# Attention in a fused layer kernel: how far its VectorE work is written ahead of TensorE, when its output is loaded, and k ahead of q

## The chip, the cores and the metric

The kernel runs on one core of a Trainium2 chip. A core has TensorE (PE, matrix products into the PSUM banks), VectorE (DVE), ScalarE (ACT), GpSimd (POOL), a sync engine (SP) whose queue starts most transfers, and 16 DMA engines. Each engine works through its own queue in order; they meet at semaphores. The metric is the device time of one execution in microseconds, the median of several runs.

## The reference

With x of 2048 x 512 (one batch), D = 512, 32 heads of 16, F = 1792, all in float32:

```python
xn = layernorm(x)
q, k, v = split(xn @ wqkv)
idx = pos[:, None] - 2 * arange(8)[None, :]
logits = einsum("hsd,hswd->hsw", q, k[idx]) * 0.25
logits = where(idx >= 0, logits, -1e9)
o = einsum("hsw,hswd->hsd", softmax(logits), v[idx])
s = o @ wo
h = relu(xn @ w1 + b1) ** 2
out = x + s * silu(h @ w2 + b2)
```

So each position looks at eight keys only: its own and every second one before it, back to 14. That part is done on VectorE; the four matrix products are done on TensorE.

## The kernel before

**Precision.** A matrix product takes three passes: operands are split into a high part (a rounded copy, ScalarE, `high`) and a low part (a subtraction on VectorE or GpSimd, `low`), and high x high, high x low and low x high are added in PSUM (`PASSES`, L34). A product of 128 x 512 by 512 x 512 is 12 matmuls.

**First phase (L522-642).** Sixteen tiles of 128 rows are normalised (`mean`, `spread`, `norm`), transposed (`trans`), split (`lowx`) and multiplied by q, k and v weights (`qkv(t, s)`; s = 0, 1, 2 for q, k, v). `evacuate` (L472) copies a product to an SBUF tile; after every second tile the pair is written to DRAM (`sq`, `sk`, `sv`) and `done_tiles` notes how many tiles there are, with q and k under one name. The FFN weights are loaded (`load_w`, L364) and split (`split_w`, L373, low part on GpSimd) as the phase goes on.

**Second phase (L645-806).** Four chunks c of 512 rows; in each, 14 steps f over F: `up(c, f)` (12 matmuls to a bank `ph`, of which `psH` has two), relu and two squares on ScalarE, `lowh(f)` (the subtraction `h<-ph,h` on VectorE, which frees the bank), and two steps later `down(pb, f, j)` for the chunk's four row tiles (12 matmuls). `gate` adds b2 and takes silu, `out_product` multiplies the attention's output by wo, `finish` multiplies and adds x and stores.

**Attention (L221-343).** A generator, `stream`, in 8 units u of 256 rows. For a unit: four times `qk` (multiply, reduce), `soft_a`, the exponential on ScalarE, `soft_b`, four times `av` (multiply, reduce into the v tile), `store` to DRAM (`so`). In its order qk of unit u stands before av of unit u - 1. There is one buffer each for q, k and v, loaded from DRAM on ScalarE's queue (`load_u`, L199); v of the last unit uses k's buffer.

**Order.** The program is one list per engine, laid out when it is built. Two planned clocks, `clock["PE"]` and `clock["V"]`, grow by prices (L43, L55-64). `pump(margin)` (L348) writes attention instructions into VectorE's list as long as their price fits under `clock["PE"] + margin`; `not_before` moves VectorE's clock to a time that it has to wait for. `defer` and `flush` (L213-219) put the load of a unit into ScalarE's list when TensorE's clock passes a time: `BEHIND` = 5000 ns after VectorE's clock for q, k, v and for the exponential, and at least `LAND` after the tiles were done; `LOAD` is how long the plan takes a load to need (`there`, L241). In the second phase the margin is `ROOM` = 1000 for chunks 1 to 3 and -500 for chunk 0 (L770), and -500 wherever `pump()` stands alone.

**The attention's output.** `load_o(u)` (L660) starts four transfers of unit u's output into the one buffer `oq`, on SP. If the unit isn't written yet, its loop (L661-663) pumps with a margin large enough to write it all, there and then. It stands at f == 7 for unit 2c and at f == 12 for unit 2c + 1 (L755, L765). `trans_o` (VectorE transpose, ScalarE copy) follows for the chunk's first two tiles at f == 10, for the other two at f == 3 of the next chunk; `lowo` one step later, `out_product` at the chunk's end (L772) and at f == 5 and 6. In the last chunk all is done at its end (L787-806).

At a chunk's end (L772-786): two output products, the last two `down` groups, `up(c+1, 0)`, `up(c+1, 1)`, then on VectorE the four gates, `lowh(0)`, `lowh(1)`, and only then `pump()`.

Of the kernel before, what the change touches and what calls it, by code (L numbers as in the profile page):

```python
# [14 lines left out]
P = 128  # L15
# [26 lines left out]

MATMUL, TRANSPOSE, DVE_FIXED, SLACK, LATE, ROOM = 227, 150, 170, 500, 3000, 1000  # L43

BEHIND, LAND, LOAD = 5000, 6000, 9500


@with_exitstack
def body(ctx: ExitStack, tc: tile.TileContext, x, wqkv, wo, w1, b1, w2, b2, out):
# [59 lines left out]
    def high(hi, lo, src):  # L109
        A.activation(hi, src, AF.Copy)  # L110
# [43 lines left out]
    def wq_parts(s, kt):  # L154
        return wq[s][:, 0, kt], wq[s][:, 1, kt], raws[s, kt]

    load_x(0)
    load_wq(0, 0)
    load_x(1)
    for kt in range(1, KT):  # L160
        load_wq(0, kt)
    for kt in (0, 2):
        load_wq(1, kt, "pr")
    load_x(2)
# [30 lines left out]

    done_tiles = dict(qk=[0, {}], v=[0, {}])
    done_units = [0]
# [23 lines left out]
    def attention():  # L221
# [5 lines left out]
        def qk(u, s):  # L227
            i0 = 2 * s
            yield from there("k", u)
            q, k, L = tiles["q", u], tiles["k", u], Ls[u]  # L230
            yield 2350
# [240 lines left out]
    def evacuate(t, s, ps):  # L472
# [4 lines left out]
        if t % 2:  # L477
            r0 = (t - 1) * P + (0 if s == 0 else HALO)
            dst = (sq, sk, sv)[s][:, r0:r0 + UP, :].rearrange("g (p e) c -> p g (e c)", e=2)
            dma(dst, stgs[s].rearrange("p g e c -> p g (e c)"))  # L480
            done = done_tiles["qk" if s < 2 else "v"]
            done[0] = t + (s > 0)
            done[1][t // 2] = clock["PE"]
# [40 lines left out]
    moments(0, sts[0])  # L524
    high(*wq_parts(0, 0))
    norm(0)
# [6 lines left out]
    moments(1, sts[1])  # L533
    low(*wq_parts(0, 0), V)

# [5 lines left out]
    for kt in range(1, KT):  # L541
        split(*wq_parts(0, kt), V)
    high(xt[0][:, 0], None, x0.rearrange("p (k n) -> p k n", k=KT))
    ps = psA("pq0_0")
    for kt in range(KT):
        if kt == KT - 1:
            trans(1)
        PE.matmul(ps, x0[:, kt * P:(kt + 1) * P], raws[0, kt], start=kt == 0, stop=kt == KT - 1)
# [12 lines left out]
    spread(3)  # L561
    qkv(0, 1, lambda: highs(2, 0))
    trans(2)
# [3 lines left out]
    mean(4)  # L567
    qkv(1, 1, lambda: highs(2, 2))
    lows(2, 2)
    spread(4)  # L570
    constants()
    trans(3)
# [86 lines left out]

    def load_o(u):  # L660
        while done_units[0] <= u:  # L661
# [52 lines left out]
    for c in range(NCH):  # L714
        last = c == NCH - 1
        pb = [psA(f"pb{c}_{j}") for j in range(TPC)]
        t0 = c * TPC
        for f in range(2, NF):
            if c == 0:
# [54 lines left out]
        pump()  # L774
        if not last:
            for i in range(2):
                for j in range(TPC):
                    down(pb, NF - 2 + i, j)
                pump()
            for i in range(2):  # L780
                up(c + 1, i)
            for j in range(TPC):
                gate(c, j, pb)
            lowh(0)
            lowh(1)
            pump()
        else:  # L787
# [40 lines left out]
```

## Time and profile before

| | us |
|---|---|
| median of 3 runs | 519.23 |
| lowest, highest | 518.88, 520.03 |
| profiled execution | 518.02 |
| its span (first to last instruction) | 516.2 |

The profile is of one execution. Its page gives busy shares by engine; the timeline lists instructions with start, duration, count and, in brackets, the idle time before them with what ended it; the windows give busy time, the granted TensorE clock and the DMA share for stretches of the span. Tile names follow the program: `ph` and `h` of the FFN, `pb` its second product, `pw` the output product, `pr`, `L`, `pv` of the attention, `oq`, `pT`, `oT` of its output. All instructions carry line 78, that of the helper that records them.

### The profile page before, as it was taken

Reading aid. Unit: us, or ns where it says so; the run is one execution under the profiler, and the core shown is the slowest. Engines: PE = TensorE matmul, PEld = TensorE weight load, DVE = VectorE, ACT = ScalarE, POOL = GpSimd, SP = SyncE. Lnnn points to the kernel's source line nnn. Section 1 sums busy time; section 2 is a strip of 40 time slices with the busy share of each in tenths; the row PEclk is TensorE's granted clock in tenths of the full one; section 3 lists DMA queues with packets and bytes.
Section 4 is the critical chain, followed back from the end, with each engine's and each line's share of the span. In section 5 each row is a group of like instructions: output and inputs, shape, how many; then the busy total and the mean of one; then the engine's idle time right before and its main releaser. Section 6 shows DMA issues by size and latency. Waiting matters only on the chain.

```text
span 516.2 us, 5907 instructions
## 1 busy us (share of the span) xinstructions
PE 493.7 (96%) x2174; PEld 403.8 (78%) x2174; DVE 425.1 (82%) x350; ACT 218.8 (42%) x397; POOL 91.9 (18%) x121
## 2 busy tenths in 40 slices
PE   8999999999999999999999999999999999949965
PEld 5788888878887888888888888888888888738854
DVE  6419992999999999976999994899998399956956
ACT  5974573852343565217242413722431642403212
POOL 1321153531002697001030000102000101100000
PEclk9999999999999999999999999999999999979998
DMA  8989869869997936443061440708046320320222
GB/s 290 278 271 362 250 184 332 245 235 326 327 290 199 290 116 224 149 171 115 9 215 60 152 163 1 234 16 255 5 153 253 104 81 22 132 81 2 81 81 83
DMA packets 48088, 88.27 MB, mean 171 GB/s; under 512 B 5324, under 2 KB 31932, under 8 KB 45244
## 3 DMA queue, kind: packets, MB, share of 16 engines
q1 hardware_dynamic: 43740, 54.34, 34.0%
q10 hardware_dynamic: 4320, 33.56, 18.4%
q8 instruction: 17, 0.28, 0.2%
q14 instruction: 11, 0.09, 0.1%
HBM read 57.94 MB, written 27.32 MB: 165 GB/s over the span
## 4 chain that ended last, share of the span: by engine, by line
PE 62%; DVE 19%; DMA 6%; issue 5%; ACT 5%; POOL 1%; SPq 0%; ACTq 0%; DVEq 0%; POOLq 0%
PE pb L78 24%; PE ph L78 23%; PE pq L78 10%; PE pw L78 5%; DVE pv L78 4%; DVE pr L78 3%; DVE L L78 3%; DVE v L78 3%; DMA xb<-xn 2%; DMA sx<-xt 2%; DVE z L78 1%; DVE h L78 1%; DMA w1r<-in_B_w 1%; ACT scratch L78 1%; DVE oT L78 1%
## 5 line engine op out<-in xcount | busy, mean ns | idle before, releaser
L78 PE MATMUL pb<-w,h 128*128 128x512 f32 x672 | 160.9, 389 | 2.5 <-DVE h L78 2.5
L78 PEld LDWEIGHTS pb<-w,h 128*128 128x128 f32 x672 | 126.0, 188 | 29.1 <-DVE h L78 2.9
L78 PE MATMUL ph<-xU,w 128*128 128x512 f32 x504 | 122.3, 394 | 8.4 <-DVE h L78 8.4
L78 ACT ACTIVATE ph<-ph,b1t 128x512 f32<-128x512 f32 x56 | 37.0, 660 | 204.1 <-PE ph L78 193.2
L78 PEld LDWEIGHTS ph<-xU,w 128*128 128x128 f32 x504 | 95.5, 190 | 29.5 <-DVE h L78 9.7
L78 PE MATMUL pq<-wq,xt 128*128 128x512 f32 x432 | 99.0, 390 | 0.8 <-DVE xt L78 0.8
L78 PEld LDWEIGHTS pq<-wq,xt 128*128 128x128 f32 x432 | 80.9, 188 | 18.5 <-DVE xt L78 1.3
L78 DVE TENSOR_TENSOR pr<-k,q 128x2048 f32<-128x2048 f32 x32 | 75.7, 2366 | 13.5 <-DMA k<-sk 13.2
L78 DVE TENSOR_TENSOR pv<-v,L 128x2048 f32<-128x2048 f32 x32 | 74.3, 2322 | 0.6
L78 DVE TENSOR_REDUCE L<-pr 128x128 f32<-128x2048 f32 x32 | 72.9, 2279 | 0.7
L78 DVE TENSOR_REDUCE v<-pv 128x256 f32<-128x2048 f32 x32 | 72.9, 2280 | 0.6
L78 DVE TENSOR_TENSOR h<-ph,h 128x512 fp32r<-128x512 f32 x56 | 38.1, 684 | 34.7 <-ACT ph L78 34.7
L78 POOL TENSOR_TENSOR z<-z,xr 128x512 f32<-128x512 f32 x12 | 19.3, 1618 | 221.1 <-DVE z L78 163.3
L78 PE MATMUL pw<-wot,oT 128*128 128x512 f32 (+2 forms) x216 | 46.8, 371 | 1.4 <-DVE oT L78 1.4
L78 PEld LDWEIGHTS pw<-wot,oT 128*128 128x128 f32 x216 | 38.0, 188 | 8.9 <-DVE oT L78 1.8
L78 PE MATMUL ph<-xT,w 128*128 128x512 f32 x168 | 40.6, 391 | 0.5 <-DVE h L78 0.5
L78 ACT ACTIVATE stg<-pq 128x512 f32<-128x512 f32 x48 | 28.1, 594 | 28.5 <-PE pq L78 25.8
L78 PEld LDWEIGHTS ph<-xT,w 128*128 128x128 f32 x168 | 31.5, 188 | 7.5 <-DVE h L78 0.9
L78 POOL TENSOR_TENSOR w<-w1r,w 128x512 fp32r<-128x512 f32 x14 | 25.2, 1798 | 63.0 <-DMA rwo<-in_A_wo 46.6
L78 ACT ACTIVATE h<-ph 128x512 fp32r<-128x512 f32 x56 | 33.6, 601 | 1.8
L78 ACT ACTIVATE ph<-ph 128x512 f32<-128x512 f32 x56 | 33.3, 595 | 0.0
L78 PE MATMUL pq<-wq,xT 128*128 128x512 f32 x132 | 32.4, 400 | 0.0
(64 smaller groups left out, 302.7 us busy)
## 6 DMA issues: line engine op xcount, KB each, us to landing
k<-sk ACTq DMA_DIRECT2D x8, 1408.0 KB, 8.5
v<-sv ACTq DMA_DIRECT2D x8, 1408.0 KB, 8.0
sx<-xt SPq DMA_DIRECT2D x12, 512.0 KB, 8.4
xU<-sx ACTq DMA_DIRECT2D x6, 1024.0 KB, 6.2
x<-in_A_x SPq DMA_DIRECT2D x16, 256.0 KB, 4.6
sq<-stg SPq DMA_DIRECT2D x8, 512.0 KB, 6.1
sk<-stg SPq DMA_DIRECT2D x8, 512.0 KB, 5.5
sv<-stg SPq DMA_DIRECT2D x8, 512.0 KB, 6.2
```

The lines of the kernel that those rows point to most:

```text
L78: return tc.keep_in_program_order(f(*a, **k))
```

## The change

Constants: `ROOM0` = 500 for chunk 0 and `ROOM` = 3500 for the others; loads of q, k and v are deferred by `FREE` = 2000 instead of `BEHIND` = 5000 (the exponential keeps 5000); `LOAD` is 11500. The first two tiles' k products come before their q products, `done_tiles` keeps q and k apart, and q, k and v are loaded each for itself, k first. The first two FFN weights are loaded and split in the opening, the low part on VectorE. `load_o(u, force)` does nothing if the unit is loaded, or not written yet and not forced. At a chunk's end one output product stays, the other follows the next chunk's first two `up`; the gates stand before those, and the stream is pumped with `room` between the pieces.

```diff
-MATMUL, TRANSPOSE, DVE_FIXED, SLACK, LATE, ROOM = 227, 150, 170, 500, 3000, 1000
+MATMUL, TRANSPOSE, DVE_FIXED, SLACK, LATE, ROOM0, ROOM = 227, 150, 170, 500, 3000, 500, 3500
-BEHIND, LAND, LOAD = 5000, 6000, 9500
+BEHIND, FREE, LAND, LOAD = 5000, 2000, 6000, 11500
...
     load_x(0)
-    load_wq(0, 0)
+    load_wq(1, 0)
     load_x(1)
     for kt in range(1, KT):
-        load_wq(0, kt)
+        load_wq(1, kt)
     for kt in (0, 2):
-        load_wq(1, kt, "pr")
+        load_wq(0, kt, "pr")
...
-    done_tiles = dict(qk=[0, {}], v=[0, {}])
+    done_tiles = {n: [0, {}] for n in "qkv"}
...
             yield from there("k", u)
+            yield from there("q", u)
...
-            while done_tiles[names][0] < 2 * (u + 1):
-                yield None
-            def start():
-                for n in names:
+            for n in names:
+                while done_tiles[n][0] < 2 * (u + 1):
+                    yield None
+                def start(n=n):
                     tiles[n, u] = load_u(n, u)
                     landing[n, u] = clock["PE"] + LOAD
-            defer(max(clock["V"] + BEHIND if u else 0, done_tiles[names][1][u] + LAND), start)
-        yield from load(0, "qk")
-        yield from load(0, "v")
+                defer(max(clock["V"] + FREE if u else 0, done_tiles[n][1][u] + LAND), start)
+        yield from load(0, "kqv")
...
-                yield from load(u + 1, "qk")
+                yield from load(u + 1, "kq")
...
-    def split_w(f):
+    def split_w(f, eng=G):
         for i, r in enumerate(raws.pop(f)):
-            split(w12[f][:, 0, i], w12[f][:, 1, i], r, G)
+            split(w12[f][:, 0, i], w12[f][:, 1, i], r, eng)
...
-    evacuate(0, 0, ps)
-    highs(1, 0)
-    lows(1, 0)
+    evacuate(0, 1, ps)
+    highs(0, 0)
+    lows(0, 0)
     mean(2)
     clock.update(PE=12000.0, V=12500.0)
-    qkv(1, 0, lambda: highs(1, 2))
+    high(*wq_parts(0, 2))
+    V.tensor_copy(wq_parts(0, 3)[0], wq_parts(0, 3)[2])
+    qkv(1, 1)
     spread(2)
-    lows(1, 2)
+    lows(0, 2)
     mean(3)
     norm(2)
+    constants()
+    for f in range(2):
+        load_w(keep, f)
     spread(3)
-    qkv(0, 1, lambda: highs(2, 0))
+    qkv(0, 0, lambda: highs(2, 0))
...
-    qkv(1, 1, lambda: highs(2, 2))
+    qkv(1, 0, lambda: highs(2, 2))
...
     lowx(3)
+    split_w(0, V)
     pump(LATE)
     qkv(1, 2)
     norm(5)
+    split_w(1, V)
     pump(LATE)
...
-            if 0 <= f < NKEEP:
+            if 2 <= f < NKEEP:
                 load_w(keep, f)
-            if 0 <= f - 1 < NKEEP:
+            if 2 <= f - 1 < NKEEP:
                 split_w(f - 1)
...
-    def load_o(u):
+    def load_o(u, force):
+        if u in oqs or (done_units[0] <= u and not force):
+            return
         while done_units[0] <= u:
...
+        room = ROOM if c else ROOM0
...
             elif f == 2:
                 finish(t0 - 4, G)
+            elif f == 3:
                 finish(t0 - 3, G)
-            elif f == 3:
                 load_r(t0 - 2)
...
-            if f == 7:
-                load_o(c * 2)
+            if f == 2 and c:
+                load_o(c * 2 - 1, True)
+            elif f >= 7:
+                load_o(c * 2, f >= 9)
...
-            if f == 12:
-                load_o(c * 2 + 1)
+            if f >= 12:
+                load_o(c * 2 + 1, last and f > 12)
...
-            pump(ROOM if c else -SLACK)
+            pump(room)
             lowh(f)
-        for j in range(2):
-            out_product(t0 + j, psT(f"pw{t0 + j}"))
-        pump()
+        out_product(t0, psT(f"pw{t0}"))
+        if last:
+            out_product(t0 + 1, psT(f"pw{t0 + 1}"))
+        pump(room)
         if not last:
             for i in range(2):
                 for j in range(TPC):
                     down(pb, NF - 2 + i, j)
-                pump()
+                if i == 0:
+                    pump(room)
+            pump()
+            not_before(clock["PE"])
+            for j in range(TPC):
+                gate(c, j, pb)
             for i in range(2):
                 up(c + 1, i)
-            for j in range(TPC):
-                gate(c, j, pb)
-            lowh(0)
-            lowh(1)
-            pump()
+                pump(ROOM)
+                lowh(i)
+            out_product(t0 + 1, psT(f"pw{t0 + 1}"))
+            pump(ROOM)
```

More of the change, by code (lines that the diff above doesn't have):

```diff
@@ L480, in evacuate @@
             dma(dst, stgs[s].rearrange("p g e c -> p g (e c)"))
-            done = done_tiles["qk" if s < 2 else "v"]
-            done[0] = t + (s > 0)
+            done = done_tiles["qkv"[s]]
+            done[0] = t + 1
             done[1][t // 2] = clock["PE"]
@@ L524, in body @@
     moments(0, sts[0])
-    high(*wq_parts(0, 0))
+    high(*wq_parts(1, 0))
     norm(0)
@@ L533, in body @@
     moments(1, sts[1])
-    low(*wq_parts(0, 0), V)
+    low(*wq_parts(1, 0), V)
     x0 = scratch(0)
@@ L541, in body @@
     for kt in range(1, KT):
-        split(*wq_parts(0, kt), V)
+        split(*wq_parts(1, kt), V)
     high(xt[0][:, 0], None, x0.rearrange("p (k n) -> p k n", k=KT))
-    ps = psA("pq0_0")
+    ps = psA("pq0_1")
     for kt in range(KT):
@@ L547, in body @@
             trans(1)
-        PE.matmul(ps, x0[:, kt * P:(kt + 1) * P], raws[0, kt], start=kt == 0, stop=kt == KT - 1)
+        PE.matmul(ps, x0[:, kt * P:(kt + 1) * P], raws[1, kt], start=kt == 0, stop=kt == KT - 1)
     lowx(1)
     low(xt[0][:, 0], xt[0][:, 1], x0.rearrange("p (k n) -> p k n", k=KT), V)
-    evacuate(0, 0, ps)
-    highs(1, 0)
-    lows(1, 0)
+    evacuate(0, 1, ps)
+    highs(0, 0)
+    lows(0, 0)
     mean(2)
     clock.update(PE=12000.0, V=12500.0)
-    qkv(1, 0, lambda: highs(1, 2))
+    high(*wq_parts(0, 2))
+    V.tensor_copy(wq_parts(0, 3)[0], wq_parts(0, 3)[2])
+    qkv(1, 1)
     spread(2)
-    lows(1, 2)
+    lows(0, 2)
     mean(3)
     norm(2)
+    constants()
+    for f in range(2):
+        load_w(keep, f)
     spread(3)
-    qkv(0, 1, lambda: highs(2, 0))
+    qkv(0, 0, lambda: highs(2, 0))
     trans(2)
@@ L567, in body @@
     mean(4)
-    qkv(1, 1, lambda: highs(2, 2))
+    qkv(1, 0, lambda: highs(2, 2))
     lows(2, 2)
     spread(4)
-    constants()
     trans(3)
```

## The prediction

> **What bounds the kernel now.** I read the page first (span, engine shares, chain of waits), then TensorE's timeline for idle time, then VectorE's timeline at those places, then windows. The page:
>
> ```profile
> span 516.2 us, 5907 instructions
> PE 493.7 (96%) x2174; PEld 403.8 (78%) x2174; DVE 425.1 (82%) x350; ACT 218.8 (42%) x397; POOL 91.9 (18%) x121
> PE 62%; DVE 19%; DMA 6%; issue 5%; ACT 5%; POOL 1%; SPq 0%; ACTq 0%; DVEq 0%; POOLq 0%
> ```
>
> TensorE is busy 96%, and none of its matmuls goes. Only its idle and slowed time, some 20 us, can be won. TensorE's timeline shows where (start, duration, count, idle before and releaser):
>
> ```profile
> 444.82 2.88 PE L78 MATMUL ph<-xU,w 128*128 128x512 f32 x12
> 447.54 2.88 PE L78 MATMUL pb<-w,h 128*128 128x512 f32 x12
> 458.82 4.58 PE L78 MATMUL ph<-xU,w 128*128 128x512 f32 x12 [8.40 <-DVE h L78]
> 463.25 2.89 PE L78 MATMUL pb<-w,h 128*128 128x512 f32 x12
> ...
> 490.46 1.29 PE L78 MATMUL pb<-w,h 128*128 128x512 f32 x5
> 494.23 7.36 PE L78 MATMUL pb<-w,h 128*128 128x512 f32 x31 [2.48 <-DVE h L78]
> 503.02 7.08 PE L78 MATMUL pw<-wot,oT 128*128 128x512 f32 x48 [1.43 <-DVE oT L78]
> ```
>
> A group of 12 matmuls advances by 447.54 - 444.82 = 2.72 us, so a step (`up` and `down`) takes 5.44 us. Three waits stand in the last chunk, and TensorE ends at 503.02 + 7.08 = 510.10, 6.1 us before the span does. What VectorE did then:
>
> ```profile
> 440.76 0.68 DVE L78 TENSOR_TENSOR h<-ph,h 128x512 fp32r<-128x512 f32 x1
> ...
> 441.95 2.28 DVE L78 TENSOR_REDUCE v<-pv 128x256 f32<-128x2048 f32 x1
> ...
> 455.88 2.29 DVE L78 TENSOR_REDUCE v<-pv 128x256 f32<-128x2048 f32 x1
> 458.09 1.28 DVE L78 TENSOR_TENSOR h<-ph,h 128x512 fp32r<-128x512 f32 x2
> ...
> 491.29 2.29 DVE L78 TENSOR_REDUCE v<-pv 128x256 f32<-128x2048 f32 x1
> 493.50 1.28 DVE L78 TENSOR_TENSOR h<-ph,h 128x512 fp32r<-128x512 f32 x2
> 500.82 1.32 DVE L78 STREAM_TRANSPOSE pT<-oq 128x512 f32<-128x512 f32 x2 [6.05 <-DMA oq<-so]
> 502.27 1.29 DVE L78 TENSOR_TENSOR oT<-pT,oT 128x512 fp32r<-128x512 f32 x2
> ...
> 513.25 0.29 DVE L78 TENSOR_TENSOR z<-z,xlast 128x128 f32<-128x128 f32 x1
> ```
>
> The reader should see a run of attention from 441.95 to 458.17 with no `h` in it. At f == 7 `load_o(6)` wants unit 6, whose attention is late, and its loop (L661-663) writes all of it in one piece. `lowh(7)` and `lowh(8)` stand behind it, and `up(3, 9)` needs the bank that `lowh(7)` frees. `load_o(7)` at f == 12 does the same until 493.58; then store, load, transpose and split take until 503.56, and the last output products wait. The attention is late, although VectorE idles 18% of the span. The windows (busy us of PE, PEld, DVE, ACT, POOL, then clock) tell where:
>
> ```profile
> 227.00:240.00 13.00, 13.00 (x58) 10.54 (x57) 4.37 (x8) 8.61 (x14) 2.54 (x2) 1.00 0.09 35
> 314.00:327.00 13.00, 13.00 (x58) 10.53 (x57) 5.71 (x7) 9.13 (x14) 2.56 (x2) 1.00 0.24 81
> 401.00:420.00 19.00, 19.00 (x85) 15.51 (x84) 9.96 (x11) 11.35 (x19) 2.55 (x2) 1.00 0.34 105
> 461.00:462.00 1.00, 1.00 (x4) 0.72 (x4) 0.00 (x0) 0.00 (x0) 0.00 (x0) 0.50 0.00 0
> 494.00:498.00 4.00, 3.77 (x16) 3.11 (x17) 0.78 (x2) 0.00 (x0) 0.00 (x0) 1.00 0.42 150
> ```
>
> At the three chunk ends VectorE idles 13 - 4.37 = 8.6, 13 - 5.71 = 7.3 and 19 - 9.96 = 9.0 us, 25 together. The last two rows are clocks: after the 8.40 us wait TensorE ran at 0.50, so its next group took 4.58 instead of 2.88; after the 2.48 us wait it ran at 1.00. The Trainium skill (TensorE: Matmul & The Clock Gate, Part 1: The HAM clock gate) says that an idle window of about 3.4 us halves the clock; the trace agrees on both sides. By it, a stall of 3 us left over would cost its own length alone.
>
> **The change part by part.**
>
> *Attention ahead (ROOM 3500, chunk ends, `load_o` when done).* Nothing is added or removed; VectorE's order changes. What there is to place:
>
> ```profile
> L78 DVE TENSOR_TENSOR pr<-k,q 128x2048 f32<-128x2048 f32 x32 | 75.7, 2366 | 13.5 <-DMA k<-sk 13.2
> L78 DVE TENSOR_TENSOR pv<-v,L 128x2048 f32<-128x2048 f32 x32 | 74.3, 2322 | 0.6
> L78 DVE TENSOR_REDUCE L<-pr 128x128 f32<-128x2048 f32 x32 | 72.9, 2279 | 0.7
> L78 DVE TENSOR_REDUCE v<-pv 128x256 f32<-128x2048 f32 x32 | 72.9, 2280 | 0.6
> L78 DVE TENSOR_TENSOR h<-ph,h 128x512 fp32r<-128x512 f32 x56 | 38.1, 684 | 34.7 <-ACT ph L78 34.7
> ```
>
> At a chunk end (TensorE's last `down` at T) four gates take the planned clock to T + 2.8. After `up(c+1,0)` the limit is T + 2.7 + 3.5, so one instruction of 2.3 fits ahead of `lowh(0)`; after `up(c+1,1)` and after the moved `out_product(t0+1)` one more each. Three per chunk end are 7 us, 21 over three ends, nearly all of the 25. (`psT` holds two banks, so the moved product needs no other.)
>
> Needed are less. Unit 6 ended at 458.17 and is now forced only from f == 9, at 447.54 + 2.72 = 450.3 at the earliest: 8 us sooner suffice. Unit 7: `up(3, 13)` would end at 450.3 + 4 x 5.44 + 2.72 = 474.8, two output products of 2.72 at 480.2, 36 `down` matmuls (8.16) at 488.4. From 493.58 to 503.56 the output path took 10.0, so unit 7 must end by 478.4, 15 sooner than 493.58. 21 cover both. So go the 8.40, 1.7, 2.48 and 1.43. The end also shortens: VectorE's gates queued behind the late `oT` and ran to 513.54, 3.4 after TensorE; with `oT` early each gate follows its bank, and after the last matmul stand only a multiply and an add of 0.3 each. 513.54 to 516.2 stays: 0.6 + 2.7 = 3.3 instead of 6.1, a gain of 2.8, of which I take 2.5.
>
> *What it costs.* VectorE's `lowh(f)` is now up to 2.5 us further behind `up(f)`. With the plan met, the attention stops 3.5 us past `down`'s end at most, so `lowh(f)` ends 2.72 + 3.5 + 0.7 = 6.9 after `up(f)`; `up(f+2)` wants the bank at 8.16. A margin of 1.3 at worst, and every lag of the real VectorE behind the plan beyond 1.3 is a TensorE wait, once, since the wait itself takes the lag away. Chunk 0 shows such lag:
>
> ```profile
> 181.87 2.97 DVE L78 TENSOR_TENSOR pr<-k,q 128x2048 f32<-128x2048 f32 x1
> 192.90 0.68 DVE L78 TENSOR_TENSOR h<-ph,h 128x512 fp32r<-128x512 f32 x1
> 194.05 2.88 PE L78 MATMUL ph<-xT,w 128*128 128x512 f32 x12
> 183.06 2.94 POOL L78 TENSOR_TENSOR w<-w1r,w 128x512 fp32r<-128x512 f32 x1 [0.36 <-DMA xr<-in_A_x]
> 185.96 1.29 POOL L78 TENSOR_TENSOR w<-w2r,w 128x512 fp32r<-128x512 f32 x1
> ```
>
> There `lowh(8)` ended at 193.58, 0.47 before `up(0, 10)`. ROOM0 is 1 us more than the old limit: all else equal, 0.5 is lost. In chunks 1 to 3 the lag is not shown with this room: bounds from nothing to 3 us in all; I take 0.7, near nothing, because VectorE there is the one that waits (34.7 us for `ph` in the last row above). The lengthening above is VectorE and GpSimd on SBUF at once (2.97 for 2.37, 2.94 for 1.29). The Trainium skill (SBUF — State Buffer, SBUF: two separate sides) calls it an exclusive lock between a VectorE instruction with two SBUF inputs and a GpSimd instruction; the trace agrees. It speaks against this change: by it GpSimd's 12 `z` adds could each delay a `lowh` written later.
>
> *Loads sooner (FREE 2000, LOAD 11500, k first).*
>
> ```profile
> 72.30 1.85 ACTq L78 DMA_DIRECT2D k<-sk  x1
> 87.26 2.29 DVE L78 TENSOR_TENSOR pr<-k,q 128x2048 f32<-128x2048 f32 x1 [9.04 <-DMA k<-sk]
> so<-v SPq DMA_DIRECT2D x8, 512.0 KB, 3.0
> oq<-so SPq DMA_DIRECT2D x32, 128.0 KB, 4.7
> 26.00:40.00 14.00, 14.00 (x66) 11.35 (x65) 1.74 (x3) 10.48 (x23) 3.50 (x12) 1.00 0.86 292
> 111.56 24.52 PE L78 MATMUL pq<-wq,xt 128*128 128x512 f32 x106 [0.84 <-DVE xt L78]
> ```
>
> The second k took 15.0 us to use against 9.5 planned: a lag of 5.5 carried into chunk 0. Issued 3 sooner and planned at 11.5 it is 0 to 3.5, which pays for ROOM0; gain 0 to 6 us of VectorE, none of TensorE's. Issuing v 2 us after the last reduce puts ScalarE's queue before a store of 3.0: it waits 1 to 2 us, and the next relu stands behind it. ScalarE is busy 42% of the span, so over 2 of a step's 5.44 us are free, and I price it at nothing; uncovered it is 2 us of `lowh` each time, within the 0 to 3. The wait of `trans_o` at f == 3 behind a load at f == 2 (4.7) arises only where a unit isn't done at f == 13; with 21 us in hand it is. In the first phase two splits (4 subtractions of 0.68) pass from GpSimd to VectorE, which was busy 1.74 of 14 us there; ScalarE's four copies move into 3.5 idle us. Nothing, or 2.7 us of attention. TensorE's longest first-phase wait is the 0.84 of the last row, behind a subtraction that later k loads (DMA share 0.86 and more) could delay: bounds -1 to +2, taken as 0.
>
> **Sum.** 8.4 + 1.7 + 2.5 + 1.4 + 2.5 - 0.7 = 15.8 us. The profiled execution took 518.02 us (span 516.2 and 1.8 around it), 1.2 below the median of the runs, 519.23. 519.2 - 15.8 = 503.4; k's earlier start makes the first-phase waits rather shorter, and I round to 503.
>
> **Rivals.** (1) *Given back in part*: `lowh` behind attention, or behind a late gate, makes TensorE wait 1 to 2.5 us at each of the three chunk ends, 3 to 7 in all: 506 to 510. For it: the margin of 1.3; against: waits take the lag away. (2) *It doesn't do what it says*: unit 6 or 7 still forced. Unit 6 needs 8 of 21 us, so this takes two chunk ends that gain nothing; half of the 15.8 remains: 511 to 516. (3) *Slower*: attention written to the limit stretches each step. 36 steps of chunks 1 to 3 hold one `lowh` (0.68) and some 2.06 instructions of attention; at the 2.31 of the groups that is 5.44, no wait. Each microsecond of step beyond 5.44 is waited for 36 times; 15.8 are used up at 0.44 per step, an instruction of 2.53. At 2.60 it is 0.6 x 36 = 21.6: 525. The 2.97 above has that size, but with GpSimd at work all the time, which chunks 1 to 3 haven't.
>
> **Chances.** Forecast (500 to 506) 0.73, rival 1 0.15, rival 2 0.05, rival 3 0.04; 0.03 for a first phase that gains more than 3. The range reaches from 499.5 (no cost, first-phase waits gone) to 509.5. A measurement of this kernel tells 0.2%, 1 us, from no change. Faster 0.92, same 0.03, slower 0.05.
>
> **What would show it.** Right: no attention run over 5 us without an `h` in the last chunk; no TensorE wait above 1 us after 160; clock 1.00 to the end; VectorE busy through the chunk ends; the last reduce of v before 478 on that timeline; 3 to 4 us after TensorE's end. Wrong: waits `PE ph <- DVE h` in chunks 1 to 3, a gap between two `down` groups at a chunk end, or `load_o` still followed by an unbroken run.

## The result and the profile after

| | before | after |
|---|---|---|
| median | 519.06 (4 runs) | 497.84 (4 runs) |
| lowest, highest | 518.76, 520.03 | 497.80, 498.13 |
| profiled execution | 518.02 | 497.80 |
| its span | 516.2 | 496.0 |

The ratio is 0.9589 [0.9573, 0.9606]: 21.2 us faster. The forecast was 503.0, and the time lies 1.7 us below the range's lower end. The direction and all the large terms came out as worked; the surplus of some 5 us is what had to be explained. (One execution each of e3 and e13 below, and one of the kernel before beside e9 to e12, ran at a strongly lowered clock and is left out of the numbers here.)

The page of the changed kernel: the span, the busy shares, and the chain of work that ended last.

```profile
span 496.0 us, 5914 instructions
PE 490.1 (99%) x2174; PEld 403.5 (81%) x2174; DVE 426.5 (86%) x355; ACT 219.7 (44%) x396; POOL 92.8 (19%) x117
PEclk9999999999999999999999999999999999999999
PE 96%; DMA 1%; DVE 1%; ACT 0%; POOL 0%; issue 0%; SPq 0%; DVEq 0%
```

The chain ran 62% of the span through TensorE and 19% through VectorE; now it is 96% TensorE. VectorE's busy time hardly moved (425.1 to 426.5): its work is the same, in another order. TensorE's timeline (start, duration, count) over the stretch where the three waits stood:

```profile
442.23 2.88 PE L78 MATMUL ph<-xU,w 128*128 128x512 f32 x12
444.95 2.88 PE L78 MATMUL pb<-w,h 128*128 128x512 f32 x12
447.67 2.88 PE L78 MATMUL ph<-xU,w 128*128 128x512 f32 x12
...
472.15 5.60 PE L78 MATMUL pw<-wot,oT 128*128 128x512 f32 x24
477.59 8.32 PE L78 MATMUL pb<-w,h 128*128 128x512 f32 x36
485.75 6.95 PE L78 MATMUL pw<-wot,oT 128*128 128x512 f32 x48
```

No row carries a bracket. The group at 447.67 stands for the one that began at 458.82 after 8.40 us idle; it starts 2.72 after the group ahead of it. TensorE ends at 492.70, 3.3 before the span. Why no `ph` waits can be seen on VectorE's timeline for the same stretch:

```profile
450.80 2.29 DVE L78 TENSOR_TENSOR pv<-v,L 128x2048 f32<-128x2048 f32 x1
453.00 0.68 DVE L78 TENSOR_TENSOR h<-ph,h 128x512 fp32r<-128x512 f32 x1
453.61 1.31 DVE L78 STREAM_TRANSPOSE pT<-oq 128x512 f32<-128x512 f32 x2
454.82 2.24 DVE L78 TENSOR_REDUCE v<-pv 128x256 f32<-128x2048 f32 x1
457.84 0.69 DVE L78 TENSOR_TENSOR h<-ph,h 128x512 fp32r<-128x512 f32 x1 [0.78 <-ACT ph L78]
458.45 1.28 DVE L78 TENSOR_TENSOR oT<-pT,oT 128x512 fp32r<-128x512 f32 x2
463.28 0.69 DVE L78 TENSOR_TENSOR h<-ph,h 128x512 fp32r<-128x512 f32 x1 [3.55 <-ACT ph L78]
```

The last reduce of v ends at 457.06; before it ended at 493.58. From there on VectorE waits for ScalarE, and every `h` comes as soon as it can. Where the time was won shows in the windows over the three chunk ends (length, then busy us of PE, PEld, DVE, ACT, POOL, clock, DMA share, GB/s), laid at the same place of each chunk as before:

```profile
222.00:235.00 13.00, 13.00 (x59) 10.77 (x58) 11.86 (x10) 7.56 (x14) 1.97 (x1) 1.00 0.26 102
309.00:322.00 13.00, 13.00 (x59) 10.78 (x58) 11.41 (x9) 6.69 (x12) 1.93 (x1) 1.00 0.05 20
396.00:415.00 19.00, 19.00 (x85) 15.74 (x84) 17.35 (x16) 9.20 (x17) 2.59 (x2) 1.00 0.14 36
```

VectorE's busy time there was 4.37, 5.71 and 9.96; it is 11.86, 11.41 and 17.35. That is 7.5, 5.7 and 7.4 more, 20.6 together, where 3 x 7 = 21 were forecast. By its store to DRAM, unit 6 came 25.3 us sooner (432.9 for 458.2), and in e2 below, which has the opening of before, at 434.6. How such an end looks on VectorE's timeline, at the third one:

```profile
394.19 2.72 DVE L78 TENSOR_TENSOR z<-pb,b2t 128x512 f32<-128x512 f32 x4 [1.03 <-PE pb L78]
396.83 2.28 DVE L78 TENSOR_REDUCE L<-pr 128x128 f32<-128x2048 f32 x1
400.72 0.69 DVE L78 TENSOR_TENSOR h<-ph,h 128x512 fp32r<-128x512 f32 x1 [1.62 <-ACT ph L78]
401.33 2.28 DVE L78 TENSOR_TENSOR pr<-k,q 128x2048 f32<-128x2048 f32 x1
403.53 0.69 DVE L78 TENSOR_TENSOR h<-ph,h 128x512 fp32r<-128x512 f32 x1
404.13 2.28 DVE L78 TENSOR_REDUCE L<-pr 128x128 f32<-128x2048 f32 x1
```

Behind the four gates stand an attention instruction, `h`, another, `h`, another: the three of the forecast, in stretches in which VectorE had waited.

**Where the 20.2 us of span went.** The starts of the same groups in both traces, subtracted, give every piece. They are of one execution each; how far the small early ones vary is said with e2. Three of the pieces lie before the last chunk, where the forecast had none, so their rows of before are needed too. First TensorE's timeline of before (the last row is one run of 36 matmuls at the first chunk end):

```profile
135.92 2.94 PE L78 MATMUL ph<-xT,w 128*128 128x512 f32 x12
...
155.84 3.01 PE L78 MATMUL ph<-xT,w 128*128 128x512 f32 x12 [0.47 <-DVE h L78]
...
226.69 8.50 PE L78 MATMUL ph<-xU,w 128*128 128x512 f32 x36
235.03 2.88 PE L78 MATMUL pb<-w,h 128*128 128x512 f32 x12
```

The same two `ph` groups in the changed kernel:

```profile
134.59 2.94 PE L78 MATMUL ph<-xT,w 128*128 128x512 f32 x12
...
153.88 2.88 PE L78 MATMUL ph<-xT,w 128*128 128x512 f32 x12
```

And the weight loads of before, on a timeline of their own (a group's first load starts some 0.2 us ahead of its first matmul, as at 135.69 for the `ph` at 135.92, so a wait for `h` falls on the load first):

```profile
232.17 2.59 PEld L78 LDWEIGHTS ph<-xU,w 128*128 128x128 f32 x12 [0.30 <-DVE h L78]
319.39 2.60 PEld L78 LDWEIGHTS ph<-xU,w 128*128 128x128 f32 x12 [0.30 <-DVE h L78]
406.61 2.60 PEld L78 LDWEIGHTS ph<-xU,w 128*128 128x128 f32 x12 [0.30 <-DVE h L78]
```

The 36 matmuls from 226.69 to the next start at 235.03 took 8.34 where three groups of 12 take 8.16: 0.18 lost at each chunk end, without a bracket on any matmul row.

| piece, by TensorE's starts | worked out as | us | in the sum |
|---|---|---|---|
| first phase: first `ph` | 135.92 - 134.59 | 1.33 | 0 |
| chunk 0: fourth `ph` | (155.84 - 153.88) - 1.33 | 0.63 | 0 (0.5 lost, paid by the sooner loads) |
| from there to the `ph` at 444.82: three chunk ends of 0.18, the rest behind the wait of 0.47 | (444.82 - 442.23) - 1.96 | 0.63 | 0 |
| the wait of 8.40 | (458.82 - 444.82) - (447.67 - 442.23) | 8.56 | 8.4 |
| the slowed group | (463.25 - 458.82) - 2.72 | 1.71 | 1.7 |
| the two waits at the end | (503.02 - 490.46) - (485.75 - 477.59) | 4.40 | 3.9 |
| last products | 7.08 - 6.95 | 0.13 | 0 |
| behind TensorE's end | 6.1 - 3.3 | 2.80 | 2.5 |
| cost of `h` behind attention | no wait in chunks 1 to 3 | 0 | -0.7 |
| sum | | 20.2 | 15.8 |

### The profile page after: what moved, and what is told of

The parts are those of the page before. It is cut to its first block, busy times and chain, and to the rows that moved or that the text cites. A ratio compares the mean times of both kernels' runs of the same rounds, so it can differ in the third digit from the quotient of the medians.

```text
span 496.0 us, 5914 instructions
## 1 busy us (share of the span) xinstructions
PE 490.1 (99%) x2174; PEld 403.5 (81%) x2174; DVE 426.5 (86%) x355; ACT 219.7 (44%) x396; POOL 92.8 (19%) x117
## 4 chain that ended last, share of the span: by engine, by line
PE 96%; DMA 1%; DVE 1%; ACT 0%; POOL 0%; issue 0%; SPq 0%; DVEq 0%
PE ph L78 31%; PE pb L78 31%; PE pq L78 25%; PE pw L78 9%; DMA x<-in_A_x 1%; PE pxT L78 0%; POOL rs L78 0%; DVE wq L78 0%; ACT xn L78 0%; DVE st L78 0%; DVE xT L78 0%; ACT stg L78 0%; DVE z L78 0%; ACT scratch L78 0%; SPq L146 0%
## 5 line engine op out<-in xcount | busy, mean ns | idle before, releaser
L78 PE MATMUL ph<-xU,w 128*128 128x512 f32 x504 | 120.6, 389 | 0.0
L78 DVE TENSOR_TENSOR pr<-k,q 128x2048 f32<-128x2048 f32 x32 | 75.9, 2372 | 1.2 <-DMA q<-sq 0.7
L78 POOL TENSOR_TENSOR z<-z,xr 128x512 f32<-128x512 f32 x12 | 21.3, 1775 | 218.1 <-DVE z L78 191.7
L78 POOL TENSOR_TENSOR w<-w1r,w 128x512 fp32r<-128x512 f32 x12 | 21.8, 1816 | 64.2 <-DMA rwo<-in_A_wo 46.1
```

The source lines that it names most:

```text
L78: return tc.keep_in_program_order(f(*a, **k))
```

## The experiments

The first theory, A, is that of the prediction: the second phase's order (margin, chunk ends, release of `load_o`) brings the attention forward, and the two forced runs go with it. Its rival, B, is that the sooner loads of the opening do it, by giving VectorE a head start. Later runs ask what the margin costs, and which edit of the opening removes the waits up to chunk 0. All ratios are against the kernel before on the same chip.

**e1: the opening alone.** The opening's hunks on the kernel before, with its margins, chunk ends and `load_o`.

```diff
-BEHIND, LAND, LOAD = 5000, 6000, 9500
+BEHIND, FREE, LAND, LOAD = 5000, 2000, 6000, 11500
...
-    load_wq(0, 0)
+    load_wq(1, 0)
...
```

> The opening alone: k ahead of q, loads deferred by 2 us and planned at 11.5, each tensor loaded for itself, first two weight splits early; margins, chunk ends and load_o as before. Theory A (the second phase's order does the work, the opening only takes the small first-phase waits of about 2 us and VectorE's lag of 5.5 us): unit 6 is still written in one forced run at f == 7 of the last chunk, 11 instead of 16 us long; time 508 to 514. Theory B (the earlier loads are what puts the attention ahead): 500 to 503.

Measured: 516.29 (515.88 to 516.91), 0.996 [0.9945, 0.9975]. Its TensorE timeline:

```profile
456.48 5.49 PE L78 MATMUL ph<-xU,w 128*128 128x512 f32 x12 [8.41 <-DVE h L78]
...
492.89 8.86 PE L78 MATMUL pb<-w,h 128*128 128x512 f32 x31 [2.48 <-DVE h L78]
```

Both expected ranges were missed: 8.41 and 2.48 stand as before (8.40 and 2.48). VectorE was ahead (its store of unit 0 started at 118.6 for 122.8, of unit 3 at 278.0 for 280.4), but the order of its list is laid out from planned clocks when the program is built. In both traces VectorE's instructions stand in the same order from 73 us to the end. A real head start moves nothing in it: the forced piece is as long, and only its place in time shifts. The 2.1 us that e1 won (518.4 - 516.29) are about those of the first phase, whose first `ph` started at 134.35 for 135.92, and of chunk 0. B falls.

**e2: the second phase alone.** The changed kernel with the opening of before.

```diff
-BEHIND, FREE, LAND, LOAD = 5000, 2000, 6000, 11500
+BEHIND, LAND, LOAD = 5000, 6000, 9500
...
-    load_wq(1, 0)
+    load_wq(0, 0)
...
```

> The second phase's part alone (margins 500 and 3500, chunk ends, load_o when done); the opening as before. Theory A: 2 to 2.6 us above the changed kernel, since only the first-phase waits and the lag in chunk 0 come back: 499.8 to 500.5, no TensorE wait over 0.3 us after chunk 0. Theory B: 508 or more, with a forced run left in the last chunk.

Measured: 499.54 (498.70 to 501.76), 0.9643 [0.9613, 0.9674]. A holds, 0.3 us below its range: 518.4 - 499.54 = 18.9 of the 21 us are here, and e1's 2.1 are the rest. No wait is left behind chunk 0; the two early ones are:

```profile
111.10 24.53 PE L78 MATMUL pq<-wq,xt 128*128 128x512 f32 x106 [0.26 <-DVE xt L78]
155.40 3.01 PE L78 MATMUL ph<-xT,w 128*128 128x512 f32 x12 [0.49 <-DVE h L78]
```

They make up its distance to the changed kernel: its first `ph` started at 135.46, 0.87 later, and the wait of 0.49 with what hangs on it is 0.65 by the starts (155.40 - 153.88 - 0.87); its profiled span is 497.6, 1.6 over 496.0. The two early waits aren't the same in every execution: the opening of before has 0.84 and 0.47 in the kernel before, 0.26 and 0.49 here and 0.45 and 1.07 in e7. So their worth, 1.33 and 0.63 in the table, is that of one pair of executions. And the wait in chunk 0 is no longer here than before (0.49 for 0.47), although ROOM0 = 500 is in: the wider margin by itself was not seen to lose anything there.

**e3: `load_o` forced at its old places**, the rest as changed.

```diff
-            if f == 2 and c:
-                load_o(c * 2 - 1, True)
-            elif f >= 7:
-                load_o(c * 2, f >= 9)
+            if f == 7:
+                load_o(c * 2)
...
-            if f >= 12:
-                load_o(c * 2 + 1, last and f > 12)
+            if f == 12:
+                load_o(c * 2 + 1)
```

> The changed kernel with load_o as before: forced at f == 7 and f == 12. Theory A: unit 6 ended at 433 and unit 7 at 457 in the changed kernel, before f == 7 (437) and f == 12 (464) of the last chunk, so nothing is left to force: 497.6 to 498.2. Theory C (loading when done is itself worth microseconds, because the forced runs come back without it): 501 or more.

Measured: 497.50, 497.70 and 499.83; 0.9613 [0.9587, 0.9638]. Forcing costs nothing once the attention is early: there is nothing left to force. Its 355 instructions on VectorE stand in the changed kernel's order, one for one. So the release of `load_o`, a part of the change, pays nothing that could be measured here.

**e7: the release of `load_o` alone**, on the kernel before.

```diff
-    def load_o(u):
+    def load_o(u, force):
+
+        if u in oqs or (done_units[0] <= u and not force):
+            return
...
-            if f == 7:
-                load_o(c * 2)
+            if f == 2 and c:
+                load_o(c * 2 - 1, True)
+            elif f >= 7:
+                load_o(c * 2, f >= 9)
...
```

> The kernel before with only load_o changed (when done; forced at f == 9, f == 13 and f == 2 of the next chunk). Two steps more of planned attention (4 instructions, 9 us) come before the force, so of the run of 16 us at f == 7 some 7 are left at f == 9. Theory A: the 8.4 wait falls to nothing or 2 us and the clock stays at 1.00, the end stays late: 508 to 513. If forcing alone were to blame for all (theory C): 500 to 503.

Measured: 515.6 (514.93 to 516.48), 0.993 [0.9904, 0.9956], outside the expected range. TensorE's timeline:

```profile
468.73 4.61 PE L78 MATMUL ph<-xU,w 128*128 128x512 f32 x12 [1.80 <-DVE h L78]
...
491.95 8.64 PE L78 MATMUL pb<-w,h 128*128 128x512 f32 x28 [5.91 <-DVE h L78]
```

The wait of 8.40 fell to 1.80, as expected, but the clock didn't stay at 1.00 behind it (last section). And the same amount of attention is still late, and the force at f == 13 pays for it in the next place: 2.48 became 5.91. Releasing the deadline alone moves most of the debt: 4.1 us were won (519.68 - 515.6), of the 21.

**e4: the old chunk ends**, the rest as changed.

```diff
-        out_product(t0, psT(f"pw{t0}"))
-        if last:
-            out_product(t0 + 1, psT(f"pw{t0 + 1}"))
-        pump(room)
+        for j in range(2):
+            out_product(t0 + j, psT(f"pw{t0 + j}"))
+        pump()
...
             for i in range(2):
                 up(c + 1, i)
-                pump(ROOM)
-                lowh(i)
-            out_product(t0 + 1, psT(f"pw{t0 + 1}"))
-            pump(ROOM)
+            for j in range(TPC):
+                gate(c, j, pb)
+            lowh(0)
+            lowh(1)
+            pump()
```

> The changed kernel with the chunk ends as before (both output products, no attention between the two up groups and the gates behind them); margins 500 and 3500 kept. Theory A with its sum of 7 us of VectorE per chunk end: unit 6 ends some 20 us later, at 453, so it is forced from f == 9 (448) for a few us and unit 7 ends near 478: 499 to 504, and the 0.2 us wait at each chunk end is back. Theory D (the margin of 3500 alone puts the attention ahead): within 0.8 of the changed kernel, 497.8 to 498.6.

Measured: 503.65 (503.19 to 503.82), 0.9714 [0.9699, 0.9728], as expected. The windows over its first two chunk ends (columns as above), and the wait that came:

```profile
222.00:235.00 13.00, 13.00 (x58) 10.56 (x57) 6.84 (x9) 6.62 (x11) 0.36 (x1) 1.00 0.26 101
309.00:322.00 13.00, 13.00 (x58) 10.56 (x57) 4.80 (x8) 6.13 (x10) 0.00 (x0) 1.00 0.07 28
```

```profile
488.22 7.08 PE L78 MATMUL pw<-wot,oT 128*128 128x512 f32 x48 [1.16 <-DVE oT L78]
```

VectorE is idle at the chunk ends again (6.84 and 4.80 busy for 11.86 and 11.41), unit 6 is stored at 451.0 instead of 432.9, and the output is late at the end: the last products start 2.47 later than in the changed kernel, take 7.08 for 6.95, and 6.1 us stand behind TensorE's end again (488.22 + 7.08 to 501.4) for 3.3. That is the 5.4 of its span over 496.0. The small waits at the chunk ends are back on the weight loads (0.30 at each), as expected; a wait of a `ph` behind a forced run at f == 9, which was expected too, didn't come.

**e5: the old margins**, the chunk ends as changed.

```diff
-MATMUL, TRANSPOSE, DVE_FIXED, SLACK, LATE, ROOM0, ROOM = 227, 150, 170, 500, 3000, 500, 3500
+MATMUL, TRANSPOSE, DVE_FIXED, SLACK, LATE, ROOM0, ROOM = 227, 150, 170, 500, 3000, -500, 1000
```

> The changed kernel with the old margins, -500 in chunk 0 and 1000 in the others, at the chunk ends too. By the plan's arithmetic nothing then fits between the two up groups of a chunk end (5.16 wanted, 3.72 allowed), so theory A says that the chunk ends gain next to nothing without the margin: unit 6 ends after 447 and is forced at f == 9, a TensorE wait returns, 502 to 510. Theory D2 (the place of the pumps matters, not the margin): within 1 us of the changed kernel.

Measured: 504.82 (504.12 to 506.73), 0.9727 [0.9697, 0.9757], as expected. TensorE's timeline:

```profile
482.92 6.68 PE L78 MATMUL pb<-w,h 128*128 128x512 f32 x28 [0.85 <-DVE h L78]
491.76 8.68 PE L78 MATMUL pw<-wot,oT 128*128 128x512 f32 x48 [2.16 <-DVE oT L78]
```

Unit 6 is stored at 451.8, as in e4. The new places at the chunk ends are there, but VectorE's timeline at the third one shows them empty:

```profile
396.78 2.48 DVE L78 TENSOR_TENSOR z<-pb,b2t 128x512 f32<-128x512 f32 x4
402.62 0.69 DVE L78 TENSOR_TENSOR h<-ph,h 128x512 fp32r<-128x512 f32 x1 [3.37 <-ACT ph L78]
405.34 0.69 DVE L78 TENSOR_TENSOR h<-ph,h 128x512 fp32r<-128x512 f32 x1 [2.03 <-ACT ph L78]
```

Nothing stands between the gates and the two `h`: under a margin of 1 us the plan put no attention there. The two edits need each other to bring the attention all the way forward: each without the other leaves unit 6 some 18 to 19 us later than both together do. In time less hangs on it: with the opening and the release of `load_o` beside it, each still keeps 15 of the 21 us (518.4 - 503.65 = 14.8 in e4, 519.68 - 504.82 = 14.9 in e5). The waits of TensorE that are left in the second phase are 1.16 in e4 and 0.32, 0.85 and 2.16 in e5.

**e6: a margin far over the bank's slack.**

```diff
-MATMUL, TRANSPOSE, DVE_FIXED, SLACK, LATE, ROOM0, ROOM = 227, 150, 170, 500, 3000, 500, 3500
+MATMUL, TRANSPOSE, DVE_FIXED, SLACK, LATE, ROOM0, ROOM = 227, 150, 170, 500, 3000, 500, 9000
```

> The changed kernel with a margin of 9000 in chunks 1 to 3: lowh may now end 2.72 + 9.0 + 0.7 = 12.4 us after its up group, 4.3 past the 8.16 at which the next but one up wants the bank. Theory A (a TensorE wait takes the lag away and is paid once): one wait or a few that add to 4 to 5 us in the first full chunk, 501 to 504. Theory E (paid in every step, rival 3 of the prediction): several us in each of 36 steps, 530 and more. Theory F (VectorE's real times stay so far ahead of plan that nothing is paid): below 498.5.

Measured: 500.94 (499.79 to 501.86), 0.9645 [0.9616, 0.9675]; profiled span 498.0. All its waits of TensorE after the first phase:

```profile
230.61 3.06 PE L78 MATMUL ph<-xU,w 128*128 128x512 f32 x12 [0.58 <-DVE h L78]
...
242.76 3.01 PE L78 MATMUL ph<-xU,w 128*128 128x512 f32 x12 [0.94 <-DVE h L78]
```

Two waits, both in the first chunk with the wide margin, none in the two chunks after it. 5.5 us more of margin cost 2.0 us of span, once, in the profiled execution, which was the fastest of four; by the medians it is 3.1 (500.94 - 497.84). Theory A had 4 to 5 and a time from 501 on, so its size was too large. A wait takes the lag away, as the prediction had it; the slower rival, in which 36 steps each pay, falls.

**e8: q ahead of k**, as in the kernel before, the rest as changed.

```diff
-    load_wq(1, 0)
+    load_wq(0, 0)
...
-    qkv(0, 0, lambda: highs(2, 0))
+    qkv(0, 1, lambda: highs(2, 0))
...
```

> The changed kernel with q ahead of k in the opening, as before; all else changed. Theory A: attention starts about 2 us later, which the 20 us in hand cover; the first-phase wait of 0.84 (1.3 us of TensorE's time) comes back only if the late VectorE caused it, so 497.8 to 499.2. If k first is what pays the 1.7 us of the opening: 499.2 to 499.8 with the wait near 111 us back.

Measured: 498.12 (497.63 to 499.64), 0.9602 [0.9571, 0.9633]; no wait of TensorE at 111 or in chunk 0. k in front of q is worth nothing that could be measured.

**e9: the changed kernel again**, beside e10 to e12.

> The changed kernel once more, as the yardstick of this call: 497.6 to 498.3.

Measured: 497.83 (497.71 to 499.78), 0.9613 [0.9589, 0.9638], span 495.9.

**e10: the old times of the loads.** **e11: without the early split of the first two weights.** Each is the changed kernel with that one part undone.

```diff
-BEHIND, FREE, LAND, LOAD = 5000, 2000, 6000, 11500
+BEHIND, FREE, LAND, LOAD = 5000, 5000, 6000, 9500
```

```diff
-    for f in range(2):
-        load_w(keep, f)
...
-    split_w(0, V)
...
-    split_w(1, V)
...
-            if 2 <= f < NKEEP:
+            if 0 <= f < NKEEP:
...
```

> The changed kernel with the loads deferred by 5000 and planned at 9500, as before; k first, early splits and the second phase kept. If VectorE's wait for the second k (9.0 us before) made the first-phase TensorE waits, it is back here, with TensorE waits near 111 and 155 us: 499.0 to 500.5. If the early weight splits made them (GpSimd freed of two splits): 497.8 to 498.5.

> The changed kernel with the first two weights loaded and split as before (GpSimd, during the first phase). If the loads' timing made the first-phase waits: within 0.5 of the changed kernel and no TensorE wait after 20 us; if the early splits did: 499.0 to 500.0 with the wait near 111 us back.

Measured: e10 497.89 (497.63 to 499.59), 0.9618 [0.9591, 0.9645]; e11 497.78 (497.56 to 497.93), 0.9605 [0.9581, 0.9628]. Neither moved, and neither has an early wait of TensorE. e10's expected 499.0 to 500.5 fell, although VectorE did wait for its load there:

```profile
85.07 2.80 DVE L78 TENSOR_TENSOR pr<-k,q 128x2048 f32<-128x2048 f32 x1 [4.70 <-DMA q<-sq]
```

**e13 and e14: from the other side.** e2 with one part of the opening put in: separate loads of k and q, k first, at the old times (e13); the new times with q and k still loaded together (e14).

```diff
-        yield from load(0, "qk")
-        yield from load(0, "v")
+        yield from load(0, "kqv")
...
-                yield from load(u + 1, "qk")
+                yield from load(u + 1, "kq")
```

```diff
-BEHIND, LAND, LOAD = 5000, 6000, 9500
+BEHIND, FREE, LAND, LOAD = 5000, 2000, 6000, 11500
```

> The second phase's part, with the opening as before except that q, k and v are each loaded for itself (deferred by 5000, planned at 9500 as before). If the separate loads are what ends the first-phase waits: 497.6 to 498.2, no TensorE wait near 111 or 155 us, the first attention instruction before 38.0. If not: 499.3 to 499.8, as with the second phase's part alone.

> The second phase's part, with the opening as before except for the loads' times (deferred by 2000, planned at 11500). If an earlier second k is enough by itself: VectorE's wait for it near 87 us shrinks from 8 to 5 or less and the waits near 111 and 155 go, 497.6 to 498.3. If not: 499.0 to 499.8.

Measured: e13 497.89, 499.07, 499.62, 499.97 and 500.91, 0.9629 [0.9595, 0.9663]. By its median e13 is at e2's time, but its interval holds the changed kernel's ratio too; what speaks for e2's is that VectorE's 350 instructions stand in e2's order, one for one. e14 measured 497.78 (497.58 to 500.23), 0.9605 [0.9571, 0.9639], the changed kernel's time, with no early wait of TensorE. So the loads' times alone are enough (e14), and they aren't needed where the other edits stand (e10). What goes with the waits, over all profiles but those of e3 and e13, is how far VectorE had come: the store of unit 1 started at 168.3 in the kernel before, 167.9 in e2 and 168.7 in e7, which have the wait in chunk 0, and at 166.5 (e10) or earlier in all that haven't. 1.4 us are enough, whichever edit brings them. That the position of VectorE is the cause, and not something that goes with it, rests on these three and on no run that moved it by itself.

**e12: two small edits more**, on the changed kernel: the last tile's output product in two pieces instead of three, and the transposes of the third tile moved behind a product, since TensorE waited 0.62 there.

```diff
-    trans(2)
     norm(3)
-    lowx(2)
...
     qkv(1, 0, lambda: highs(2, 2))
+    trans(2)
     lows(2, 2)
+    lowx(2)
...
-                ends = (0, D // 2, 3 * D // 4, D) if j == TPC - 1 else (0, D)
+                ends = (0, D // 2, D) if j == TPC - 1 else (0, D)
```

> The changed kernel with two edits for what its profile still shows: the last product in two pieces of 256 columns instead of 256, 128 and 128 (a piece of 128 took 1.34 us of TensorE, as long as one of 256; 1.34 saved, about 0.5 given back in a longer last multiply, add and store), and the transpose of tile 2 one product later (0.62 wait at 17.5). Theory A: 0.8 + 0.6 = 1.4 below the changed kernel, 496.2 to 496.8. Rival: the 0.62 only moves to another wait: 0.5 to 0.9 below.

Measured: 496.93 (496.44 to 498.54), 0.9591 [0.9567, 0.9616]; profiled span 494.7, 1.2 under e9's on the same chip, 0.9 by medians. The intervals of the two overlap, so only the traces tell them apart. Its TensorE timeline:

```profile
485.02 5.75 PE L78 MATMUL pw<-wot,oT 128*128 128x512 f32 x36
```

The products take 5.75 for 6.95, and they start 0.6 earlier than e9's (485.62); of the wait of 0.62, 0.30 is left at 20.25. TensorE so ends at 490.77, 1.8 sooner than e9's 492.57; 0.6 of that goes behind it, where a piece of 256 columns is multiplied, added and stored after the last matmul (3.9 to the span's end for 3.3). The median lies 0.1 above theory A's range, and its 0.9 would fit the rival as well; the span's 1.2 stands between the two. By its median it is the fastest of all that were run.

## Why the prediction was right in the main, and where it failed

**What bounds it, and what goes: right.** All four terms that the argument rested on came out close to their size: 8.56 for 8.4, 1.71 for 1.7, 4.40 for 3.9, 2.80 for 2.5. The 21 us of attention brought forward were 20.6, and e4 and e5 show that both edits are needed to bring unit 6 so far forward. Unit 7 had to end by 478.4 and ended at 457.1. Of the signs that were named, all came true but one: no wait above 1 us, clock 1.00 to TensorE's end, VectorE busy at the chunk ends, the last reduce of v before 478, 3.3 behind TensorE's end. The sign of no attention run over 5 us without an `h` in the last chunk was set too narrow: from 422.58 to 429.51 three attention instructions, 6.9 us, stand between two `h`, and no `ph` waits. TensorE has an output product in that step, so it is 8.16 us long and not 5.44.

**The step that failed: "bounds -1 to +2, taken as 0"** for TensorE's time in the first phase, with "I take 0.7" for the cost in chunks 1 to 3 and "0.5 is lost" for ROOM0 beside it. The runs showed a gain of 1.33 in the first phase and of 0.63 in chunk 0, and nothing paid in chunks 1 to 3. The mechanism of the cost had been seen (`lowh` behind attention), but in chunk 0 its sign was that of the start: before, VectorE came into chunk 0 late enough for one `ph` to wait 0.47, and with the head start it came early enough for none. In the first phase the wait itself stood among the prediction's rows, with 0.84 of idle time, and was judged mainly as something that could grow. On the weight loads' timeline of before it is this:

```profile
111.55 2.15 PEld L78 LDWEIGHTS pq<-wq,xt 128*128 128x128 f32 x10 [1.28 <-DVE xt L78]
114.00 21.65 PEld L78 LDWEIGHTS pq<-wq,xt 128*128 128x128 f32 x96 [0.30 <-ACT stg L78]
```

The subtraction that the first load waits for started at 110.81; in the changed kernel it starts at 106.16, and the wait is gone. By starts, at the changed kernel's pace of 0.227 per matmul, TensorE lost 1.04 at this wait and 0.32 in the run behind it, where the second row's load waits for ScalarE; the run of 396 that takes their place starts 0.03 later (44.79 for 44.76). That makes the 1.33, a third more than the bound of 1 that was read from the matmul's row. The prediction also gave a reason for shorter first-phase waits, k's earlier start, and priced it at nothing; e8 shows that k ahead of q isn't needed for it, and e14 that the sooner loads are enough.

**The terms that were too small.** Five small pieces were not in the sum or short in it: the stretch of the three chunk ends (0.63; the 0.18 at each is visible only on the weight loads), the two waits at the end (0.5 over), behind TensorE's end (0.3), the wait of 8.40 (0.16) and the last products (0.13). One reason is common to two of them: a wait costs TensorE more than its idle column. The row of a group ends with its last matmul, which takes 389 ns, while the next one starts 227 ns after it when nothing is waited for; so a wait adds 0.16 to its idle time. The 8.40 cost 8.56, and the 2.48 cost 2.64. The pieces together, 1.33 + 0.63 + 0.63 + 0.5 + 0.3 + 0.16 + 0.13 + 0.7, are 4.4: 20.2 for 15.8.

**The offset of the median.** The prediction carried the 1.2 us between the profiled execution and the median over to the changed kernel. There the two agree (497.80 and 497.84). With 4.4 this makes the 5.6 by which 503.4 was missed. The kernel before spread over 515.81 to 522.33 beside the experiments, the changed one over 497.7 to 498.1 with one execution at 499.78. The profiled execution of before was one with a high mean clock, 0.991; of the 35 beside the experiments three had that (515.81 to 517.60), the others 0.982 to 0.990 (516.98 to 522.33). So the clock behind its waits very likely has a part in the spread; that it made all of it was not shown.

**The rivals.** Given back in part: no wait came at the chunk ends. Still forced: e3 shows that nothing is forced, and e4 and e5 what it looks like where the output is late again, at 503.7 and 504.8. Slower, each step paying: e6 excludes it, since even a margin 5.5 us wider is paid once.

**The two rules that were weighed.** From the page TensorE: Matmul & The Clock Gate (Part 1: The HAM clock gate) of the Trainium skill the prediction drew that a stall of 3 us costs its own length. The runs speak against that, as the last section shows. From the Trainium skill's SBUF — State Buffer (SBUF: two separate sides) it drew that GpSimd's `z` adds could delay a `lowh`. That rule is about VectorE instructions with two SBUF inputs; `lowh` reads `ph` in PSUM and only `h` in SBUF, so by it a `lowh` could be late only behind an attention multiply. The group of these adds in the changed kernel's page:

```profile
L78 POOL TENSOR_TENSOR z<-z,xr 128x512 f32<-128x512 f32 x12 | 21.3, 1775 | 218.1 <-DVE z L78 191.7
```

They took 1618 ns on average before and take 1775 now, while VectorE's attention multiplies stayed (2372 for 2366). So if the two lost time to each other, it fell on GpSimd, and no `ph` waited. The rule may hold; it cost TensorE nothing here.

## What to carry to other kernels

Where a program's order is laid out in advance, a deadline that forces late work puts all of it on an in-order engine ahead of short urgent work; moving the deadline alone mostly moves the wait (e7), and a real head start changes nothing in the order (e1), while work written into the idle stretches ahead pays. Here the margin with the chunk ends and the sooner loads paid; k ahead of q (e8), the early splits (e11) and the release of `load_o` (e3) paid nothing that could be measured beside them. How far ahead may it be written: here up to the slack of the buffers at no cost, and beyond it the overshoot was paid once, not at each step (e6). When summing such a change, look at the weight loads' waits and at start-to-start distances besides the idle column of the matmuls, and don't carry an offset between profile and median from a kernel full of waits to one without.

## What the runs showed of the hardware that was not expected

**A short wait can halve TensorE's clock.** In the kernel before the clock stayed at 1.00 after 2.48 us idle. In e1 a wait as long, at the same place of the program, halved it: 31 matmuls took 8.86 instead of 7.36, 1.5 more than the wait itself. In e7 1.80 us were enough: a group of 12 took 4.61 for 2.88, at a clock of 0.50. In e5, after 2.16, 48 matmuls took 8.68 for e4's 7.08, which came after 1.16. After waits of 1.16 and less no row is longer than 0.2 us over its like (3.06 for 2.88 in e6). So a wait between 1.8 and 2.5 us cost 1.5 to 1.7 us beyond its length, or nothing.

Which of the two it is, the traces tell. The granted clock changes only on a grid of 3.41 us: in e1 at 451.73, 461.97, 492.69, 496.11 and 509.76, which are 3, 9, 1 and 4 times 3.41 apart. Here are the windows of that grid around the wait of 2.48, first in e1, then in the kernel before (columns as above):

```profile
489.28:492.69 3.41, 1.13 (x5) 0.59 (x4) 3.38 (x3) 0.00 (x0) 0.00 (x0) 1.00 0.00 0
492.69:496.11 3.42, 3.22 (x8) 2.55 (x9) 0.74 (x2) 0.00 (x0) 0.00 (x0) 0.50 0.38 153
```

```profile
489.53:492.94 3.41, 2.22 (x10) 1.50 (x8) 3.38 (x2) 0.00 (x0) 0.00 (x0) 1.00 0.00 0
492.94:496.35 3.41, 2.12 (x9) 1.76 (x10) 1.83 (x3) 0.00 (x0) 0.00 (x0) 1.00 0.38 154
```

In e1 one window took 2.28 us of the idle time, and the clock of the next one is 0.50; in the kernel before an edge parts the wait into 1.19 and 1.29, and nothing falls. In e7 and e5 all of the 1.80 and the 2.16 lay in one window. A window with 1.55 us idle (the kernel before, from 448.57) still left the next at 1.00. So in these traces the place of a wait on the grid decides, and the border lies between 1.55 and 1.80 us idle within one window, for matmuls of 512 columns at full clock; behind the narrow last pieces the clock fell after less (1.12 in the changed kernel, when its matmuls were done). The Trainium skill (TensorE: Matmul & The Clock Gate, Part 1: The HAM clock gate) names an idle window of some 3.4 us that runs free of the program. The grid agrees with that; but a wait doesn't have to fill a window, so as a safe limit for waits the measurement decides against it.

**Narrow pieces cost TensorE.** The last tile's product in pieces of 256, 128 and 128 columns takes 48 matmuls with the others, in two pieces of 256 it takes 36 for the same columns: 6.95 and 5.75. Twelve more matmuls cost 1.20, 100 ns each, though the columns are the same: in the changed kernel's trace a matmul of 128 columns starts some 0.11 us after the one before it, one of 256 some 0.12.
